# Two pairs of small matmul steps joined, and one PSUM bank each for two kinds of small results, in a delta-rule attention kernel with two feed-forward layers

## The chip, the cores and the metric

The kernel runs on one core of a Trainium2 chip. Its time is device time in microseconds (us). The engines are TensorE (PE, matrix products; PEld is its weight load), VectorE (DVE), ScalarE (ACT), GpSimd (POOL) and the sync engine (SP), which issues the DMA transfers. PSUM, the memory into which PE writes, has eight banks; all eight are in use.

## The reference

A delta rule runs over 768 time steps for 4 batches and 8 heads of size 48, and two feed-forward layers follow.

```python
k_n = k / (norm(k) + 1e-6)
for t in range(S):                       # S = 768
    y[t]  = q[t] @ state                 # state: 48 x 48 for each batch and head
    v_old = state.T @ k_n[t]
    state = state + beta[t] * outer(k_n[t], v[t] - v_old)
x = y as (3072 tokens, 384)
h = x @ w_in;  g = where(h >= 1, h, where(h <= -1, 0, (h + 1)**2 / 4));  x = g @ w_out     # 384 -> 2048 -> 384
h = x @ w_in2; g = maximum(h, 0)**2;                                     out = g @ w_out2
```

## The kernel before

**The recurrence in chunks.** Time is cut into 24 chunks of 32 steps. A chunk's tile has 128 rows: 4 batches of 32 steps. For each chunk PE first makes gram matrices of keys with keys and queries (`gram`, L280), which are masked into `gp`. For a group of up to four chunks, `tri` (L346) inverts the triangular systems, on GpSimd for most groups: one DVE transpose opens it (L363), 60 short GpSimd operations do it (L423 and L424), one DVE transpose closes it (L427). Then `chunk_steps` (L469) does the recurrence in six steps, each 32 small matmuls (64 records in the profile), but for the last:

- `ks` (K S, L484): keys times the state; DVE subtracts it from the scaled values (L494).
- `tr` (L498): the inverse times that, which gives U; ACT copies U out (L506).
- `qs` (Q S, L484 with another index): queries times the state, into the tile `yy`; then the next load of keys and queries is issued.
- `ku` (K'U, L529): adds to the state, which stays in two PSUM banks (`sps`); DVE and ACT copy it out for the next chunk (L534, L535). The last chunk has no K'U.
- `pu` (P U, L518): adds to `yy`; ACT copies the sum out as y (L522).
- `xt` (L552): three transposes of y; ACT rounds the result to the high part (L554), DVE takes the low part (L555). They are the input of the first layer.

**The feed-forward layers.** The first layer takes the chunks in nine blocks of 2 or 3 (`SIZES`), so 256 or 384 columns. For each of 16 slices f of the inner dimension, `hidden` (L577) makes a group of nine matmuls (three products of high and low parts over three slices) and the activation, and `out1` (L626) a group of nine into three accumulators, two slices later. The second layer does the same with 512 tokens at a time.

**What sets the order.** PE's order is written out by hand: the loop at L884 issues, for each f, `hidden`, what is due in slot 2x, `out1` for an earlier slice, and what is due in slot 2x + 1. So each slot follows a group of nine wide matmuls. The chunk steps of block n are spread evenly over the 32 slots of block n - 1 (L813 to L831; over the last 13 slots for n = 1), six steps for each chunk, and four gram steps are put between the steps of some chunks. The variables `at` and `ready` keep the slots at which chunks start and grams are made; the times of `tri` follow from them. The order on DVE, ACT and GpSimd is made by a planner from the dependencies.

**Banks.** Two PSUM banks hold the state, three the accumulators of the output, one the hidden group h. The last two have one tag `att` with two buffers, and all small results (ks, tr, yy, xt and the grams) take them in turn. In the first part of the kernel, before the loop, the small results rotate over these two and the accumulators; the first groups of h, those of the first layer's last block and those of the second layer rotate over the h bank and these two.

Of the kernel before, what the change touches and what calls it, by code (L numbers as in the profile page):

```python
# [8 lines left out]
F32 = mybir.dt.float32  # L9
# [16 lines left out]
def kernel(  # L26
# [22 lines left out]
    nc = tc.nc  # L49
    NCH, P, DM = out.shape  # L50
# [29 lines left out]
    ps = ctx.enter_context(tc.tile_pool(name="ps", bufs=1, space=PSUM))  # L80
# [17 lines left out]
    s_ps = [ps.tile([P, H, D], F32, name=f"sps{i}") for i in range(B2)]  # L98


    early = ["att", "acc0", "att", "acc1", "acc2"]
    turn = [0]

    def att(shape, name):
        tag = "att"
        if turn[0] is not None:
            tag = early[turn[0] % len(early)]
            turn[0] += 1
        return ps.tile(shape, F32, tag=tag, bufs=2 if tag == "att" else 1, name=name)

    def tmp(name, bufs):
        return ring.tile([P, DM], F32, tag=name, bufs=bufs, name=name)
# [6 lines left out]
    def load_kq(c):  # L119
        if c < NCH:  # L120
            kqt[c] = fetch_kq(c, "kqt", KQ)
# [153 lines left out]
    def per_bh(f):  # L275
        for h in range(H):
            for b in range(B):
                f(b, h, slice(T * b, T * (b + 1)), slice(64 * (b % 2), 64 * (b % 2) + D))
# [43 lines left out]
    HEADS = SIZES[0]  # L322
# [146 lines left out]
    def chunk_steps(c):  # L469
        n, j = block_of[c]  # L470
        g, gj = group_of[c]
        t = {}

        def of_state(o, x):

            if c < HEADS:
                for a in range(c):
                    per_bh(lambda b, h, p, pd: nc.tensor.matmul(
                        o[p, h], cross[a, c][p, h, x], us[a][p, h],
                        start=a == 0 and h == 0, stop=x == 0 and a == c - 1,  # L480
                        skip_group_check=True,
                    ))
            else:
                per_bh(lambda b, h, p, pd: nc.tensor.matmul(  # L484
                    o[p, h], kqt[c][pd, b // 2, h, x * T:(x + 1) * T], st[pd, b // 2, h],
                    start=h == 0, stop=x == 0, skip_group_check=True,
                ))

        def ks():
            r = t["r"] = kvt[c][:, 1]  # L490
            if c:
                o = att([P, H, D], "ks")
                of_state(o, 0)
                nc.vector.tensor_sub(r, r, o)  # L494

        def tr():
            o = att([P, H, D], "tr")
            per_bh(lambda b, h, p, pd: nc.tensor.matmul(  # L498
                o[p, h], gp[g][p, 0, gj, h], t["r"][p, h],
                start=h == 0, stop=True, skip_group_check=True,  # L500
            ))
            if c >= HEADS:
                us[c] = t["r"]
            else:
                us[c] = wp.tile([P, H, D], F32, tag=spare[f"u{c}"], name="u")
            nc.scalar.copy(us[c], o)  # L506

        def qs():
            o = t["o"] = att([P, H, D], "yy")
            of_state(o, 1)  # L510
            if c >= HEADS:
                kqt.pop(c)
                load_kq(c + KQ)

        def pu():
            o = t["o"]
            y = t["y"] = t["r"]
            per_bh(lambda b, h, p, pd: nc.tensor.matmul(  # L518
                o[p, h], gp[g][p, 1, gj, h], us[c][p, h],
                start=c == 0 and h == 0, stop=True, skip_group_check=True,  # L520
            ))
            nc.scalar.copy(y, o)  # L522

        def ku():
            k_ = kvt[c]
            if c < NCH - 1:
                kf = k_.rearrange("p x h d -> p (x h d)")
                w = 64 if c == 0 else D
                per_bh(lambda b, h, p, pd: nc.tensor.matmul(  # L529
                    s_ps[b // 2][pd.start:pd.start + w, h], kf[p, D * h:D * h + w], us[c][p, h],  # L530
                    start=c == 0 and h == 0, stop=c == NCH - 2, skip_group_check=True,
                ))
                if c >= HEADS - 1:
                    nc.vector.tensor_copy(st[:, 0], s_ps[0])  # L534
                    nc.scalar.copy(st[:, 1], s_ps[1])  # L535
            done()

        def done():

            t["n"] = t.get("n", 0) + 1  # L540
            if t["n"] == 2:
                del kvt[c]
                load_kv(c + 3)

        def xt():
            if j == 0:
                xh[n] = ring.tile([P, KT, P * SIZES[n]], F32R, tag="xh", bufs=2, name="xh")
                xl[n] = ring.tile([P, KT, P * SIZES[n]], F32R, tag="xl", bufs=2, name="xl")
            o = att([P, KT, P], "xt")
            yf = t["y"].rearrange("p h d -> p (h d)")  # L550
            for kt in range(KT):
                nc.tensor.transpose(o[:, kt], yf[:, kt * P:(kt + 1) * P], ident)  # L552
            cols = slice(j * P, (j + 1) * P)
            nc.scalar.copy(xh[n][:, :, cols], o)  # L554
            marks[2] = nc.vector.tensor_sub(xl[n][:, :, cols], o, xh[n].bitcast(F32)[:, :, cols])  # L555
            done()

        return [ks, tr, qs, pu, ku, xt] if c < HEADS else [ks, tr, qs, ku, pu, xt]


    x2 = dram.tile([P, KT, NCH * P], F32, name="x2", bufs=1)
# [15 lines left out]
    def hidden(layer, n, f):  # L577
        w = P * SIZES[n] if layer == 0 else N
        xs = (xh[n][:, kt] for kt in range(KT)), (xl[n][:, kt] for kt in range(KT))
        if layer:  # L580
            xs = xh[n], xl[n]
        many = turn[0] is not None or (layer, n) >= (0, NB - 1) or n == 0 and f < MANY
        bank = "att" if many and f % 3 else "h"
        h = ps.tile([P, w], F32, tag=bank, bufs={"h": 1, "att": 2}[bank], name="h")
        wi = weight(0, f)
        cols = [slice(kt * P, (kt + 1) * P) for kt in range(KT)]
        prods([
            (h, (wi[0][:, c], wi[1][:, c]), x, kt == 0, kt == KT - 1)
            for kt, (c, *x) in enumerate(zip(cols, *xs))
        ])  # L590
        if layer == 0:
            r = ring.tile([P, w], F32, tag="rg", bufs=RG, name="r")
            g = ring.tile([P, w], F32, tag="rg", bufs=RG, name="g")
        else:
            rg = ring.tile([P, 2, w], F32, tag="xl", bufs=2, name="rg")
            r, g = rg[:, 0], rg[:, 1]
        if layer == 0:


            marks[0] = nc.scalar.activation(r, h, AF.Relu, bias=one)  # L600
            marks[1] = nc.vector.tensor_scalar(g, r, 2.0, 0.5, ALU.min, ALU.mult)  # L601
            nc.scalar.activation(g, g, AF.Square)  # L602
            nc.vector.scalar_tensor_tensor(g, r, -1.0, g, ALU.add, ALU.max)  # L603
        else:
            marks[0] = nc.scalar.activation(r, h, AF.Relu, bias=zero)  # L605
            marks[1] = nc.vector.tensor_mul(g, r, r)  # L606

        def rest():
            if layer == 0:
                ghi = ring.tile([P, w], F32R, tag="gh", bufs=GB, name="gh")  # L610
                glo = ring.tile([P, w], F32R, tag="gl", bufs=GB, name="gl")
            else:
                gg = ring.tile([P, 2, w], F32R, tag="xh", bufs=2, name="gg")
                ghi, glo = gg[:, 0], gg[:, 1]
            nc.scalar.copy(ghi, g)  # L615
            nc.vector.tensor_sub(glo, g, ghi.bitcast(F32))  # L616
            gs[layer, n, f] = (ghi, glo)

        return rest
# [150 lines left out]
    with tc.manual_schedule(engines=ENGINES):  # L770
# [32 lines left out]
        def put_a(n, slot, f):  # L803
            exa.setdefault(SL * n + slot, []).append(f)
# [8 lines left out]
        for n in range(1, NB):  # L813
            todo = []
            for c in range(FIRST[n], FIRST[n] + SIZES[n]):
                g, j = group_of[c]
                due = []
                if j == 0 and 2 <= g < NG - 1:
                    due = list(range(GFIRST[g + 1], GFIRST[g + 1] + GROUPS[g + 1]))
                for i, s_ in enumerate(chunk_steps(c)):  # L820
                    todo.append(((at, c) if i == 0 else None, s_))
                    if i and due:
                        x = due.pop(0)
                        todo.append(((ready, x), lambda x=x: gram(x)))
                assert not due
            for i, (mark, s_) in enumerate(todo):
                o = 0 if n > 1 else HEAD
                slot = SL * (n - 1) + o + i * (SL - o) // len(todo)
                if mark:
                    mark[0][mark[1]] = slot  # L830
                put_a(0, slot, s_)  # L831
# [52 lines left out]
        for x in range(total):  # L884
            g, f = divmod(x, NF)
# [64 lines left out]
```

## Time and profile before

| | us |
|---|---|
| median of 3 runs | 1042.16 |
| lowest, highest | 1041.61, 1044.85 |
| the profiled execution | 1043.48 |
| its span on the core | 1041.8 |

Busy in that span: PE 984.1 us (94%), DVE 572.2 (55%), ACT 467.1 (45%), GpSimd 319.1 (31%). The core's mean granted clock is 0.994 of full speed.

How to read the rows: times run from the start of the span. A row of the timeline has the start, the time from its first instruction's start to its last one's end, the engine, the line of the kernel, the operation, the tiles (written <- read), the shapes and the count; in brackets the idle time of the engine before it and what ended it. Matmuls are pipelined, so a row's time overlaps the next row's start; the difference of two starts is what a group takes from the engine. A small matmul step stands as 64 records.

### The profile page before, as it was taken

The page shows a single profiled execution, that of the slowest core. Times are in us where ns is not written, and L with a number is a line of the kernel's source. Part 1 is how long each engine was busy: PE and PEld are TensorE (multiplying, and loading weights), DVE is VectorE, ACT ScalarE, POOL GpSimd, SP SyncE. Part 2 cuts the span into 40 slices and gives each one's busy share as a digit, 9 for nine tenths or more (in the row PEclk, how much of TensorE's full clock was granted, in tenths as well). Part 3 has the DMA queues.
Part 4 walks back from the last instruction along what each step waited for, and adds up shares of the span by engine and source line. Part 5 has one row for each costly group of instructions (what it writes and reads, how often), then busy time and mean ns, then how long its engine had stood idle before and what let it go on. Part 6 is the DMA issues. An engine that isn't in the chain of part 4 may idle for free.

```text
span 1041.8 us, 32099 instructions
## 1 busy us (share of the span) xinstructions
PE 984.1 (94%) x14152; PEld 905.0 (87%) x14152; DVE 572.2 (55%) x994; ACT 467.1 (45%) x935; POOL 319.1 (31%) x476
## 2 busy tenths in 40 slices
PE   4358899999999999999999999999999999999998
PEld 4347888899899989999999999998989999999997
DVE  6988665775575666666546577533343333433333
ACT  2776354554454545545444554333333333333332
POOL 3792770393059118518503122120020010200000
PEclk9998999999999999999999999999999999999999
DMA  9874144441542542513012223101010000000000
GB/s 258 223 204 145 47 133 142 116 137 43 159 118 61 155 116 74 145 55 100 17 41 63 91 78 99 31 1 61 1 61 1 1 31 1 23 8 1 31 1 31
DMA packets 35245, 80.83 MB, mean 78 GB/s; under 512 B 4513, under 2 KB 15265, under 8 KB 35105
## 3 DMA queue, kind: packets, MB, share of 16 engines
q1 hardware_dynamic: 35104, 78.78, 25.6%
q8 instruction: 111, 1.82, 0.8%
q14 instruction: 30, 0.24, 0.1%
HBM read 63.03 MB, written 15.73 MB: 76 GB/s over the span
## 4 chain that ended last, share of the span: by engine, by line
PE 84%; DMA 6%; DVE 5%; ACT 2%; issue 1%; SPq 1%; ACTq 0%; DVEq 0%
PE acc L567 37%; PE h L567 37%; DMA raw<-in_w_dram 5%; PE tr L498 2%; PE yy L518 2%; PE sps L529 2%; PE yy L484 2%; PE g L293 1%; PE ks L484 1%; DVE g L603 1%; DMA kqt<-in_kq_dram 1%; PE xt L552 1%; DVE gp L427 1%; DVE wl L187 1%; DVE gm L363 0%
## 5 line engine op out<-in xcount | busy, mean ns | idle before, releaser
L567 PE MATMUL acc<-w,gg 128*128 128x384 f32 x1152 | 218.2, 337 | 0.3 <-ACT e L623 0.3
L567 PE MATMUL h<-x2s,w 128*128 128x512 f32 x864 | 213.8, 392 | 0.0
L567 PEld LDWEIGHTS acc<-w,gg 128*128 128x128 f32 x1152 | 204.5, 187 | 8.6 <-ACT e L623 0.9
L567 PEld LDWEIGHTS h<-x2s,w 128*128 128x128 f32 x864 | 160.9, 188 | 28.2
L567 PE MATMUL h<-xh,w 128*128 128x384 f32 (+1 forms) x864 | 167.2, 330 | 2.3 <-ACT r L600 1.7
L567 PE MATMUL acc<-gh,w 128*128 128x384 f32 (+1 forms) x864 | 166.7, 328 | 1.5 <-ACT gh L615 1.5
L606 DVE TENSOR_TENSOR rg<-rg 128x512 f32<-128x512 f32 x96 | 71.3, 743 | 139.5 <-ACT rg L605 139.5
L567 PEld LDWEIGHTS h<-xh,w 128*128 128x128 f32 x864 | 138.5, 192 | 7.3 <-ACT r L600 2.3
L567 PEld LDWEIGHTS acc<-gh,w 128*128 128x128 f32 x864 | 136.0, 189 | 6.5 <-ACT gh L615 1.7
L605 ACT ACTIVATE rg<-h,zero 128x512 f32<-128x512 f32 x96 | 66.0, 687 | 137.7 <-PE h L567 137.7
L616 DVE TENSOR_TENSOR gl<-g,gh 128x384 fp32r<-128x384 f32 (+1 forms) x144 | 89.1, 619 | 63.7 <-ACT gh L615 59.8
L616 DVE TENSOR_TENSOR gg<-rg,gg 128x512 fp32r<-128x512 f32 x96 | 66.7, 695 | 104.3 <-ACT gg L615 104.3
L600 ACT ACTIVATE r<-h,one 128x384 f32<-128x384 f32 (+1 forms) x144 | 78.3, 544 | 97.0 <-PE h L567 96.0
L615 ACT CAST gh<-g 128x384 fp32r<-128x384 f32 (+1 forms) x144 | 68.7, 477 | 107.1 <-DVE g L603 90.1
L424 POOL TENSOR_TENSOR tx<-tx,t 128x30 f32<-128x30 f32 (+9 forms) x180 | 110.3, 613 | 13.7
L423 POOL TENSOR_TENSOR t<-tx,gm 128x30 f32<-128x30 f32 (+9 forms) x180 | 108.5, 603 | 18.8 <-DVE tx L402 5.2
L615 ACT CAST gg<-rg 128x512 fp32r<-128x512 f32 x96 | 59.7, 622 | 119.6 <-PE acc L567 112.6
L603 DVE SCALAR_TENSOR_TENSOR g<-r,g 128x384 f32<-128x384 f32 (+1 forms) x144 | 88.3, 613 | 40.5 <-ACT g L602 38.8
L601 DVE TENSOR_SCALAR g<-r 128x384 f32<-128x384 f32 (+1 forms) x144 | 57.9, 402 | 87.7 <-ACT r L600 86.8
L567 PE MATMUL h<-xl,w 128*128 128x384 f32 (+1 forms) x432 | 91.5, 321 | 1.3 <-DVE xl L555 1.3
L567 PE MATMUL acc<-gl,w 128*128 128x384 f32 (+1 forms) x432 | 91.0, 319 | 1.8 <-DVE gl L616 1.8
L602 ACT ACTIVATE g<-g 128x384 f32<-128x384 f32 (+1 forms) x144 | 70.2, 487 | 47.9 <-DVE g L601 47.2
(98 smaller groups left out, 930.3 us busy)
## 6 DMA issues: line engine op xcount, KB each, us to landing
raw<-in_w_dram SPq DMA_DIRECT2D x64, 384.0 KB, 3.7
kqt<-in_kq_dram SPq DMA_DIRECT2D x88, 192.0 KB, 3.7
kv<-in_kv_dram SPq DMA_DIRECT2D x24, 384.0 KB, 3.2
w2f<-wl SPq DMA_DIRECT2D x32, 192.0 KB, 3.3
w2r<-w2f SPq DMA_DIRECT2D x16, 384.0 KB, 3.0
x2r<-x SPq DMA_DIRECT2D x6, 768.0 KB, 4.8
out_dram<-e SPq DMA_DIRECT2D x23, 192.0 KB, 2.0
x<-e SPq DMA_DIRECT2D x18, 192.0 KB, 2.1
```

The costliest lines, as they stand in the source:

```text
L423: eng.tensor_mul(t, by.to_broadcast(shape), of.to_broadcast(shape))
L424: eng.tensor_add(rest, rest, t)
L484: per_bh(lambda b, h, p, pd: nc.tensor.matmul(o[p, h], kqt[c][pd, b // 2, h, x * T:(x + 1) * T], st[pd, b // 2, h], start=h == 0, stop=x = ...
L567: nc.tensor.matmul(o, *((r, l) if swap else (l, r)), **flags)
L600: marks[0] = nc.scalar.activation(r, h, AF.Relu, bias=one)
L601: marks[1] = nc.vector.tensor_scalar(g, r, 2.0, 0.5, ALU.min, ALU.mult)
L602: nc.scalar.activation(g, g, AF.Square)
L603: nc.vector.scalar_tensor_tensor(g, r, -1.0, g, ALU.add, ALU.max)
L605: marks[0] = nc.scalar.activation(r, h, AF.Relu, bias=zero)
L606: marks[1] = nc.vector.tensor_mul(g, r, r)
L615: nc.scalar.copy(ghi, g)
L616: nc.vector.tensor_sub(glo, g, ghi.bitcast(F32))
```

## The change

The two buffers with one tag become two tags with a buffer each. `att1` takes `yy` alone (Q S and P U); `att0` takes all other small results. Before the loop the rotation names the same five banks as before; the groups of h that used the two buffers in turn now name them by f.

For the chunks from the third on, the six steps become four: K S and Q S together, U, K'U and P U together, and the transposes. In the second pair the copies of the state come behind both matmul steps, and the copy of y behind those. The first two chunks keep six steps. A gram may now also stand right behind the first step of a chunk.

```diff
-    early = ["att", "acc0", "att", "acc1", "acc2"]
+    early = ["att0", "acc0", "att1", "acc1", "acc2"]
     turn = [0]
 
     def att(shape, name):
-        tag = "att"
+        tag = "att1" if name == "yy" else "att0"
         if turn[0] is not None:
             tag = early[turn[0] % len(early)]
             turn[0] += 1
-        return ps.tile(shape, F32, tag=tag, bufs=2 if tag == "att" else 1, name=name)
+        return ps.tile(shape, F32, tag=tag, name=name)
...
                 start=c == 0 and h == 0, stop=True, skip_group_check=True,
             ))
-            nc.scalar.copy(y, o)
+            if c < HEADS:
+                nc.scalar.copy(y, o)
...
                     start=c == 0 and h == 0, stop=c == NCH - 2, skip_group_check=True,
                 ))
+                if c >= HEADS:
+                    pu()
                 if c >= HEADS - 1:
                     nc.vector.tensor_copy(st[:, 0], s_ps[0])
                     nc.scalar.copy(st[:, 1], s_ps[1])
+            else:
+                pu()
+            if c >= HEADS:
+                nc.scalar.copy(t["y"], t["o"])
             done()
...
-        return [ks, tr, qs, pu, ku, xt] if c < HEADS else [ks, tr, qs, ku, pu, xt]
+        return [ks, tr, qs, pu, ku, xt] if c < HEADS else [lambda: (ks(), qs()), tr, ku, xt]
...
-        bank = "att" if many and f % 3 else "h"
-        h = ps.tile([P, w], F32, tag=bank, bufs={"h": 1, "att": 2}[bank], name="h")
+        h = ps.tile([P, w], F32, tag=("h", "att0", "att1")[f % 3 if many else 0], name="h")
...
                 for i, s_ in enumerate(chunk_steps(c)):
                     todo.append(((at, c) if i == 0 else None, s_))
-                    if i and due:
+                    if due:
                         x = due.pop(0)
                         todo.append(((ready, x), lambda x=x: gram(x)))
```

## Rows read from the trace of the kernel before

**Rows 1.** The profile page's part 4: the chain that ended last, by engine

```profile
PE 84%; DMA 6%; DVE 5%; ACT 2%; issue 1%; SPq 1%; ACTq 0%; DVEq 0%
```

**Rows 2.** Busy time by stretch: length, each engine's busy us, PEclk, DMA share, GB/s

```profile
104.00:200.00 96.00, 89.00 (x2438) 81.49 (x2439) 59.26 (x127) 45.73 (x112) 41.80 (x69) 0.98 0.37 106
200.00:590.00 390.00, 388.08 (x7682) 359.26 (x7681) 238.38 (x429) 199.32 (x417) 176.91 (x273) 1.00 0.32 93
...
640.00:1041.80 401.80, 397.85 (x2003) 361.55 (x2001) 153.51 (x217) 131.01 (x208) 32.31 (x30) 1.00 0.06 22
```

**Rows 3.** PE's groups, 104 to 640 us: busy us, mean ns | idle before

```profile
L567 PE MATMUL h<-xl,w 128*128 128x384 f32 x288 | 65.9, 337 | 1.3 <-DVE xl L555 1.3
...
L484 PE MATMUL ks<-st,kqt 48*32 48x48 f32 x1408 | 19.5, 204 | 0.0
L498 PE MATMUL tr<-kv,gp 32*32 32x48 f32 x1408 | 19.4, 202 | 5.2 <-DVE kv L494 5.2
```

**Rows 4.** Timeline of PE: wide groups alone and between small steps

```profile
101.51 0.87 PE L567 MATMUL h<-xh,w 128*128 128x256 f32 x6
...
102.57 0.87 PE L567 MATMUL acc<-gh,w 128*128 128x256 f32 x6
...
126.79 0.88 PE L484 MATMUL yy<-st,kqt 48*32 48x48 f32 x64
127.60 0.97 PE L567 MATMUL h<-xh,w 128*128 128x256 f32 x6
...
128.86 0.93 PE L529 MATMUL sps<-kv 32*48 32x48 f32 x64
...
336.99 1.31 PE L567 MATMUL h<-xh,w 128*128 128x384 f32 x6
...
338.75 0.89 PE L484 MATMUL yy<-st,kqt 48*32 48x48 f32 x64
...
595.96 1.20 PE L567 MATMUL h<-xh,w 128*128 128x384 f32 x6
...
597.52 1.20 PE L567 MATMUL acc<-gh,w 128*128 128x384 f32 x6
```

**Rows 5.** Timeline of PE: two small steps back to back, before the loop

```profile
52.31 1.50 PE L498 MATMUL tr<-kv,gp 32*32 32x48 f32 x64 [2.61 <-DVE kv L494]
53.60 1.49 PE L478 MATMUL yy<-u,cross 32*32 32x48 f32 x64
```

**Rows 6.** Timeline of PE: stalls, and a slow step at 113.22

```profile
110.57 0.88 PE L498 MATMUL tr<-kv,gp 32*32 32x48 f32 x64 [2.03 <-DVE kv L494]
...
113.22 1.50 PE L484 MATMUL yy<-st,kqt 48*32 48x48 f32 x64
...
124.72 0.88 PE L498 MATMUL tr<-kv,gp 32*32 32x48 f32 x64 [0.83 <-DVE kv L494]
...
170.10 0.88 PE L498 MATMUL tr<-kv,gp 32*32 32x48 f32 x64 [1.73 <-DVE kv L494]
...
194.79 0.79 PE L567 MATMUL h<-xl,w 128*128 128x384 f32 x3 [0.58 <-DVE xl L555]
```

**Rows 7.** Timeline: DVE's transpose and read-out of ks, then xt and its read-out

```profile
107.35 2.11 DVE L427 STREAM_TRANSPOSE gp<-tx 128x1024 f32<-128x1024 f32 x1
...
109.98 0.54 DVE L494 TENSOR_TENSOR kv<-kv,ks 128x384 f32<-128x384 f32 x1
...
164.78 0.49 PE L552 MATMUL xt<-ident,kv 128*128 128x128 f32 x3
...
168.26 0.57 DVE L555 TENSOR_TENSOR xl<-xt,xh 128x384 fp32r<-128x384 f32 x1
```

**Rows 8.** Timeline: end of one GpSimd chain, and DVE's transpose of its result

```profile
341.28 0.28 POOL L424 TENSOR_TENSOR tx<-tx,t 128x30 f32<-128x30 f32 x1
...
349.15 2.22 DVE L427 STREAM_TRANSPOSE gp<-tx 128x1024 f32<-128x1024 f32 x1
```

**Rows 9.** Busy time of the stretch behind the first stall

```profile
110.50:116.00 5.50, 5.43 (x146) 5.02 (x146) 2.12 (x7) 1.61 (x5) 4.10 (x11) 0.69 0.06 13
```

## The prediction

> **What bounds the kernel now.** I read the chain of waits first: TensorE (PE) holds 84% of it, and nearly all of the rest lies in the first 100 us, where data and constants come in [rows 1]. The table by stretches says the same in time. From 104 to 200 us PE is busy 89.0 of 96.0 us, from 200 to 590 us 388.1 of 390.0, and from 640 us on 397.9 of 401.8; VectorE (DVE) is busy for 238.4 of the 390 [rows 2]. So from 104 us on, a microsecond counts if it is one of PE's own or if PE stands still for it. Before that PE waits for others; the change leaves the order of work there as it is (the rotation over five banks names the same banks), so I put that stretch at zero. After 640 us nothing is touched.
>
> Next I read PE's groups from 104 to 640 us. The recurrence steps are short: all of K S takes 19.5 us. The counts give the number of steps: 1408 records of ks are 22 chunks of 64 (the first two chunks are done earlier). PE's idle time is small: 5.2 us ahead of tr and 1.3 us ahead of h [rows 3], of 8.9 us in all between 104 and 590 us (7.0 and 1.9) [rows 2].
>
> **The change, part by part.**
>
> *1. Fewer interruptions.* Each recurrence step is put into a stream of wide matmuls. In PE's order of time, a group of nine 384-wide matmuls between two others takes 595.96 to 597.52 = 1.56 us; one that has a small step on either side takes 336.99 to 338.75 = 1.76. For 256 columns it is 101.51 to 102.57 = 1.06 and 127.60 to 128.86 = 1.26 [rows 4]. Both ends of an interruption together cost 0.20 us, whatever the width. The change puts Q S right behind K S in 22 chunks and P U right behind K'U in 21 (the code does no K'U for the last chunk), so 43 interruptions go. No matmul goes: 64 records of each step stay.
>
> What the new seam between two small steps costs, the steady stretch does not show. Bounds: nothing, or the 0.20 us of a seam between small and wide. The nearest row is early, where tr and yy stand back to back: tr starts at 52.31 and yy 1.29 us later, both last 1.50 and 1.49 us, so the second is not stretched [rows 5]. PE ran at half pace there, but it is the same kind of seam, so I take nothing. Term: 43 x 0.20 = 8.6 us less, bounds 0 to 8.6.
>
> *2. Waits of PE that get more time.* A block's steps are spread over 32 slots (a slot follows each group of nine wide matmuls). Per three chunks there were 18 steps, or 22 with four gram steps; now there are 12 or 16. Two steps that lay 1.5 slots apart now lie 2 or more apart. That bears on these stalls:
> - tr waits for DVE to subtract ks: 5.2 us in five stalls, the largest 2.03 at 110.57, 0.83 at 124.72 and 1.73 at 170.10 [rows 3, 6]. Each had one group between ks and tr; now Q S (126.79 to 127.60, 0.81 us [rows 4]) lies between too, and in all but the first of them two groups or more. The first is set by DVE, which runs a 2.11 us transpose from 107.35 and gets to the subtraction at 109.98 [rows 7]; there only Q S and its seams come in between, so about 1.1 us stays. Gone: 5.2 - 1.1 = 4.1.
> - the first group of a block waits for the low part of the last transposed chunk: 1.3 us in two stalls (0.58 at 194.79) [rows 3, 6]. That xt was at slot 30 and is now at 28 or 29, a group of over 1 us earlier. Gone: 1.3.
> Term: 5.4 us less, bounds 0 (the stall comes back elsewhere) to 6.5.
>
> *3. A new wait: one bank for K S, U, xt and the grams.* Each of these had a second bank; now each waits until the result before it has been read out. Behind a waiting step PE's whole queue stands. Between two uses of the bank now lie two groups, 2.3 us at 256 columns (1.06 + 1.26) and 3.3 at 384 [rows 4]. tr needs the ks result read anyway. What is late next is K S behind xt. The worst row: xt ends at 165.27 (164.78 + 0.49) and DVE reads it out from 168.26 to 168.83, 3.56 us later [rows 7]. Before, K S ran meanwhile in the other bank. With one bank K S of that chunk would wait 3.56 - 2.3 = 1.2 us; but the read-out stood behind a transpose that closes a group, and the change places that transpose a slot behind xt instead of in the same slot, so it may fall after the read-out. Bounds 0 to 1.2; I take the middle, 0.6. At 384 columns 3.56 would exceed the gap by 0.3 us only.
>
> The Trainium skill (page Perfetto Trace Analysis, section Optimizing Tensor Performance, Matmuls) speaks against this part: independent groups of matmuls should rotate through different PSUM banks, so that one is read out while the next computes. By that rule all three uses of a chunk would pay; the rival "one bank" below prices it. The rows agree with it only where the read-out is longer than the wide groups in between.
>
> *4. Moves on the other engines.* The copy of y goes from behind P U to behind the copies of the state, on ScalarE's (ACT) queue, and xt waits for it; no copy is added. The loads of later K and Q chunks go out one step earlier on the sync queue, which helps if anything. For one group of chunks the last gram now comes three slots later, so GpSimd's chain starts later: it ended at 341.56 (341.28 + 0.28), 7.6 us before DVE transposed its result at 349.15 [rows 8]. Three slots, each a group of 1.56 to 1.76 us [rows 4] and part of an insertion, are some 6 us, of which merging gives back about half by then, and tr of that chunk also moves two slots on; no cost. The order on DVE and ACT is planned anew, though, and a 2 us transpose can again fall ahead of a result that PE needs. I allow one such stall of the size of 1.73 us [rows 6]; bounds 0 to 4.
>
> **Sum.** -8.6 - 5.4 + 0.6 + 1.7 = -11.7 us. The profiled execution took 1043.48 us (span 1041.8), so it would take 1031.8. It lay 1.3 us above the median of the runs, 1042.16; from that median the forecast is 1030.5.
>
> Not in the sum: behind the 2.03 us stall the granted clock falls to 0.69 over 110.5 to 116 us (2.4 GHz for part of it, 1.2 for the rest) and a step that takes 0.88 us at 126.79 takes 1.50 at 113.22 [rows 4, 6, 9]. The step and its two neighbours lose some 1.5 us. If halving the stall keeps the clock up, that is a further gain; as half the stall stays, I count none.
>
> **Rivals.**
> - *Only the seams go.* The stalls move with the new plan instead of vanishing: 1042.2 - 8.6 = 1033.5. For it: the causes, DVE's 2 us transposes, all stay [rows 7]. Against: the distances grow in all chunks.
> - *The seam between small steps costs like any other.* Then part 1 is nil and parts 2 to 4 leave 1042.2 - 3.1 = 1039. For it: no row at full clock shows two small steps back to back. Against: rows 5.
> - *One bank makes it slower.* Place: the 256-wide stretches, 8 chunks, whose two groups give only 2.3 us. If DVE's queue made a delay of 3.56 us the rule there, three uses per chunk would wait 1.2 us each: 8 x 3 x 1.2 = 29 us more, less the 8.6 of part 1: 1062. It starts to decide when the bank is awaited 0.13 us per use on average (8.6 over 22 chunks x 3). For it: the 3.56 us row [rows 7]. Against: that read-out, and that of 109.98, stood behind a transpose, and the code has two of these for each of seven groups of chunks, not one ahead of every read-out.
> - *It comes out even.* The merged insertion is twice as long (1.6 us), so ACT's and DVE's work for the wide groups shifts against PE and new gaps eat the gain: 1041 to 1043. Against: DVE has 150 of 390 us free [rows 2].
>
> **How the numbers follow.** The forecast 0.60, with its own range 1026 to 1033; only the seams 0.17; dear seams 0.10; one bank slower 0.08; even 0.05. Within 0.3% (3.1 us) a measurement of this kernel can't be told from no change: faster means below 1039.0. That takes in the first two cases and half of the third: 0.82. Same: the other half and the even case, 0.10. Slower: 0.08. Range: the low end is both upper bounds of parts 1 and 2 and the clock's 1.5 us without any new stall, 1042.2 - 8.6 - 6.5 - 1.5 = 1025.6, rounded down to 1025; the high end takes in the larger part of the dear seams, 1038.5.
>
> **What would show it.** Right: in steady stretches ks starts, yy follows 0.81 us later, the next wide group 1.63 us later; sps and yy likewise; the wide groups keep 1.56, 1.66 and 1.76 us, with fewer of the last; PE's idle from 104 to 590 us falls from 8.9 to about 6 us. Wrong: yy starts over 0.9 us after ks, or the first wide matmul behind a pair is longer than behind a single step (dear seams); PE's waits name the read-outs of xt, u or g ahead of ks and g (one bank); or the time falls by less than 8 us though the seams are gone, and then PE's idle names a new wait.

## The result, and the profile after

| | median us (runs) | lowest to highest |
|---|---|---|
| before | 1042.16 (5) | 1041.23 to 1044.92 |
| changed | 1029.86 (5) | 1027.45 to 1030.92 |

The medians lie 12.3 us apart; the ratio is 0.9872 with a 95% interval of 0.985 to 0.9894 (11 to 16 us less). The forecast was 1030.5. The profiled execution of the changed kernel took 1027.45 us, its span 1025.7.

First the busy time of the changed kernel by stretches (columns as in [rows 2]). PE stands still for 5.3 us from 104 to 200 us and for 2.3 from 200 to 590, so 7.6 us against 8.9.

```profile
104.00:200.00 96.00, 90.70 (x2656) 84.75 (x2654) 63.64 (x134) 50.13 (x121) 49.58 (x80) 1.00 0.40 117
200.00:590.00 390.00, 387.70 (x7552) 368.38 (x7553) 248.39 (x441) 202.13 (x426) 173.69 (x266) 1.00 0.31 93
...
640.00:1025.70 385.70, 381.76 (x1922) 346.96 (x1921) 143.04 (x202) 124.35 (x197) 28.95 (x27) 1.00 0.05 18
```

The whole difference lies ahead of the second layer: that starts at 633.40 us before and at 617.32 now, and takes 408.4 and 408.3 us. Of these 16.1 us 1.5 are there when the first wide group starts (68.86 and 67.32), a stretch that holds the same instructions in the same order; that is scatter between two executions. 14.5 us are left to explain. (In both kernels the granted clock is at its lower level for part of the time ahead of 104 us: a mean of 0.92 over 60 to 104 us before and of 0.80 now.)

PE's groups from 104 to 640 us in the changed kernel answer to [rows 3]. The wait of tr fell from 5.2 to 1.4 us and that of h from 1.3 to nothing; a wait of ks for the read-out of xt, 3.6 us, is new.

```profile
L574 PE MATMUL h<-xl,w 128*128 128x384 f32 x288 | 65.7, 336 | 0.0
...
L484 PE MATMUL ks<-st,kqt 48*32 48x48 f32 x1408 | 19.5, 204 | 3.7 <-DVE xl L562 3.6
L498 PE MATMUL tr<-kv,gp 32*32 32x48 f32 x1408 | 19.4, 202 | 1.4 <-DVE kv L494 1.4
...
L484 PE MATMUL yy<-st,kqt 48*32 48x48 f32 x1408 | 19.1, 203 | 1.5 <-issue 1.5
```

Next PE's timeline around a chunk in the steady part of the changed kernel. Q S starts 0.71 us behind K S and the wide group 0.78 behind Q S; a single step had kept PE for 0.81. P U starts 0.86 behind K'U and keeps PE for 0.82.

```profile
304.71 0.88 PE L484 MATMUL ks<-st,kqt 48*32 48x48 f32 x64
305.42 0.86 PE L484 MATMUL yy<-st,kqt 48*32 48x48 f32 x64
306.20 1.32 PE L574 MATMUL acc<-gh,w 128*128 128x384 f32 x6
...
313.67 0.93 PE L530 MATMUL sps<-kv 32*48 32x48 f32 x64
314.53 0.88 PE L518 MATMUL yy<-kv,gp 32*32 32x48 f32 x64
315.35 1.31 PE L574 MATMUL acc<-gh,w 128*128 128x384 f32 x6
```

Over all undisturbed pairs of the trace the medians are 0.704 and 0.790 us for K S and Q S (0.814 each before), and 0.863 and 0.812 for K'U and P U (the same as before). With the interruption, 0.204, a pair of the first kind saves 2 x 0.814 - 0.704 - 0.790 + 0.204 = 0.338 us, one of the second 0.204. So by the rows the seams are worth 22 x 0.338 + 21 x 0.204 = 11.7 us.

The last piece is the clock. In the stretch of [rows 9] it now stays up:

```profile
110.50:116.00 5.50, 5.50 (x173) 5.18 (x160) 2.83 (x8) 3.25 (x8) 4.67 (x11) 1.00 0.01 3
```

The stall ahead of tr is 1.42 us here, not 2.03, and no step of this stretch takes 1.50 us:

```profile
109.76 0.88 PE L498 MATMUL tr<-kv,gp 32*32 32x48 f32 x64 [1.42 <-DVE kv L494]
```

These are some 1.5 us, which the forecast had named and left out. Together: 11.7 of seams, 8.9 - 7.6 = 1.3 of idle time, some 1.5 of clock, 14.5 us. That this meets the 14.5 exactly is in part chance. The three terms belong to the time from about 98 us on, when both kernels start the same gram:

```profile
98.25 1.10 PE L293 MATMUL g<-kqt 48*32 48x64 f32 x64
97.37 1.10 PE L293 MATMUL g<-kqt 48*32 48x64 f32 x64
```

The first row is from the kernel before, the second from the changed one. The lead is 0.9 us here, so from here on there are 16.1 - 0.9 = 15.2 us, and 0.7 of them stay without an explanation. Between the first wide group and this gram the changed kernel lost 0.7 us of its lead, with PE busy for 23.4 of 30.1 us there (24.3 of 29.4 before).

### The profile page after: what moved, and what is told of

Its sections match the earlier page's. It is cut to its first block, busy times and chain, and to the rows that moved or that the text cites. A ratio compares the mean times of both kernels' runs of the same rounds, so it can differ in the third digit from the quotient of the medians.

```text
span 1025.7 us, 32117 instructions
## 1 busy us (share of the span) xinstructions
PE 968.5 (94%) x14152; PEld 900.8 (88%) x14152; DVE 576.5 (56%) x994; ACT 465.7 (45%) x935; POOL 320.6 (31%) x476
## 4 chain that ended last, share of the span: by engine, by line
PE 84%; DMA 6%; DVE 5%; ACT 2%; issue 1%; SPq 0%; ACTq 0%; DVEq 0%
PE acc L574 38%; PE h L574 37%; DMA raw<-in_w_dram 5%; PE sps L530 2%; PE tr L498 2%; PE yy L518 2%; PE ks L484 2%; PE yy L484 1%; PE g L293 1%; DVE gp L427 1%; DVE gm L363 1%; DMA kqt<-in_kq_dram 1%; PE xt L559 1%; DVE g L609 1%; ACT r L606 1%
## 5 line engine op out<-in xcount | busy, mean ns | idle before, releaser
L574 PE MATMUL h<-xh,w 128*128 128x384 f32 (+1 forms) x864 | 161.3, 323 | 2.9 <-ACT r L606 2.3
L423 POOL TENSOR_TENSOR t<-tx,gm 128x30 f32<-128x30 f32 (+9 forms) x180 | 111.7, 621 | 16.1 <-DVE tx L402 2.8
L607 DVE TENSOR_SCALAR g<-r 128x384 f32<-128x384 f32 (+1 forms) x144 | 62.1, 431 | 73.5 <-ACT r L606 72.6
```

The costliest lines, as they stand in the source:

```text
L423: eng.tensor_mul(t, by.to_broadcast(shape), of.to_broadcast(shape))
L574: nc.tensor.matmul(o, *((r, l) if swap else (l, r)), **flags)
```

## Experiments

All times are against the kernel before, run beside it on the same chip. The ratio is turned into microseconds of 1042.

| run | median us | ratio (95%) | us against before |
|---|---|---|---|
| banks alone, six steps, old slots | 1046.38 | 1.004 (1.0025 to 1.0055) | +4.2 |
| Q S joined alone | 1035.54 | 0.9938 (0.9922 to 0.9955) | -6.5 |
| P U joined alone | 1040.83 | 0.9987 (0.9973 to 1.0) | -1.4 |
| both joined, old slots | 1037.93 | 0.9963 (0.995 to 0.9976) | -3.9 |
| new slots, nothing joined | 1040.57 | 0.9982 (0.9972 to 0.9992) | -1.9 |
| changed kernel, xt in the other bank | 1026.81 | 0.985 (0.9835 to 0.9865) | -15.6 |
| the same again | 1029.25 | 0.9872 (0.9851 to 0.9893) | -13.3 |
| changed kernel again, beside it | 1028.77 | 0.9874 (0.9853 to 0.9895) | -13.1 |
| six steps, old slots, xt in the other bank | 1043.28 | 1.0011 (0.9997 to 1.0025) | +1.1 |
| both joined, old slots, xt in the other bank | 1034.18 | 0.9922 (0.9897 to 0.9946) | -8.1 |
| xt in the other bank, grams joined | 1032.00 | 0.9901 (0.988 to 0.9922) | -10.3 |
| pairs in turned order | 1029.86 (one run) | | |

**Banks alone.** The new tags, the rest as before; `pu` is a step by itself again, with its copy. (The edits here and below are against the changed kernel; `...` stands for lines not shown.)

```diff
...
-                if c >= HEADS:
-                    pu()
...
-        return [ks, tr, qs, pu, ku, xt] if c < HEADS else [lambda: (ks(), qs()), tr, ku, xt]
+        return [ks, tr, qs, pu, ku, xt] if c < HEADS else [ks, tr, qs, ku, pu, xt]
...
-                    if due:
+                    if i and due:
```

> The new banks with the six old steps at their old slots; no pair is joined. Theory A (the time went with the seams: in the profile after, Q S starts 0.70 us behind K S instead of 0.81 and every pair saves an interruption of 0.20, so 22 x 0.34 + 21 x 0.20 = 11.7 us): no gain, 1042 us, or up to 4 us slower if K S waits for the read-out of xt. Theory B (part of the gain is fewer waits of PE through banks and spacing): the banks alone bring nothing either, 1042. Rival, banks matter: 1039 or less, or over 1046.

4.2 us slower: this is theory A's upper bound and the far end of the rival, so it does not part the two, but theory B's 1042 is out. The banks are not free. PE's waits from 104 to 640 us (us, times, longest) have a new first row, in an execution of 1048.31 us, the slowest of its seven:

```profile
PE ks L484 <- DVE xl L555: 6.1, 6, 2.5
PE tr L498 <- DVE kv L494: 3.9, 4, 2.5
```

**Only Q S joined, only P U joined.** One pair each; the other step stays alone, so chunks have five steps, at slots of their own. In the first, P U has its own copy of y again.

```diff
...
-        return [ks, tr, qs, pu, ku, xt] if c < HEADS else [lambda: (ks(), qs()), tr, ku, xt]
+        return [ks, tr, qs, pu, ku, xt] if c < HEADS else [lambda: (ks(), qs()), tr, ku, pu, xt]
```
```diff
-        return [ks, tr, qs, pu, ku, xt] if c < HEADS else [lambda: (ks(), qs()), tr, ku, xt]
+        return [ks, tr, qs, pu, ku, xt] if c < HEADS else [ks, tr, qs, ku, xt]
```

> Only Q S joined to K S; P U stays a step of its own. Theory A: 22 x 0.34 = 7.4 us less than before, 1034.8. With a seam worth 0.20 us as I forecast: 22 x 0.20 = 4.4 less, 1037.8. If waits are what counts: tr gets more time after K S, the larger part of the 5.4 us of waits goes too, 1033 or less.

> Only P U joined to K'U; Q S stays a step of its own. Theory A: 21 x 0.20 = 4.3 us less than before, 1037.9, and P U starts 0.86 us behind K'U (this seam, unlike the other, gives nothing beyond the interruption). Rival, each pair is worth the same: 5.9 us less, 1036.3.

Q S alone gives 6.5 us (4.7 to 8.1); theory A's 7.4 lies in the interval, and 4.4 does not. P U alone gives 1.4 (0 to 2.8), less than its 4.3; its waits of PE from 104 to 640 us sum to 8.9 us, no fewer than before. The seams themselves are as theory A has them in both traces (medians 0.704 and 0.863 us). But each of the two times is a sum of seams, banks and five-step slots, so neither gives the price of a seam by itself. They add up to 7.9, not to 13: in this sum the price of the banks (4.2 us at the slots of six steps) stands twice. How much of the gap is the banks and how much the slots, these two runs do not show.

**Both joined at the old slots.** Empty steps stand where Q S and P U were.

```diff
+        none = lambda: None
-        return [ks, tr, qs, pu, ku, xt] if c < HEADS else [lambda: (ks(), qs()), tr, ku, xt]
+        return [ks, tr, qs, pu, ku, xt] if c < HEADS else [lambda: (ks(), qs()), tr, none, ku, none, xt]
...
-                    if due:
+                    if i and due:
```

> Both pairs joined, but the slots of the old plan are kept (empty steps stand where Q S and P U were), so tr is again mostly one group behind K S and the grams lie where they were. Theory A (seams): 11.7 us less than before, 1030.5, as the changed kernel within 2 us. Theory B (the forecast's part 2, waits that get more time): the 5 us of waits ahead of tr stay, 1034 or more, and tr's idle time is named in PE's waits.

3.9 us, far from 11.7: the seams alone do not give the time. In the profiled execution (1041.56 us, the slowest of twelve) PE stands still for 14.6 us from 104 to 640 us, against 8.9 before. But the waits are not mainly those ahead of tr that theory B named (2.8 us): ks waits 7.2 us for xt. Two stalls come close together in PE's timeline, and the table of stretches shows the clock behind them at 0.77:

```profile
144.70 0.97 PE L575 MATMUL h<-xh,w 128*128 128x256 f32 x6 [1.39 <-ACT r L607]
147.07 1.48 PE L484 MATMUL ks<-st,kqt 48*32 48x48 f32 x64 [1.04 <-DVE xl L562]
```
```profile
145.00:160.00 15.00, 13.96 (x376) 13.09 (x375) 7.14 (x17) 7.59 (x20) 6.50 (x14) 0.77 0.43 137
```

**New slots, nothing joined.** Q S and P U one slot behind K S and K'U.

```diff
...
+        behind_[ks], behind_[ku] = qs, pu
-        return [ks, tr, qs, pu, ku, xt] if c < HEADS else [lambda: (ks(), qs()), tr, ku, xt]
+        return [ks, tr, qs, pu, ku, xt] if c < HEADS else [ks, tr, ku, xt]
...
                 put_a(0, slot, s_)
+                if s_ in behind_:
+                    put_a(0, slot + 1, behind_[s_])
```

> The slots of the changed kernel, but Q S and P U stand one slot behind K S and K'U, so a group of wide matmuls lies between and no interruption is saved (in one or two places the next step shares the slot); waits for tr and xt have the new spacing. Theory A (seams): the gain of 11.7 us is gone, 1040 to 1042. Theory B (waits): the part of 5.4 us stays, 1037 or less.

1.9 us (0.8 to 2.9): theory A's range, and not the 5.4 of the forecast. In the timeline the price of the wide groups is back (312.14 - 310.37 = 1.77 us between two small steps):

```profile
309.56 0.88 PE L485 MATMUL ks<-st,kqt 48*32 48x48 f32 x64
310.37 1.32 PE L569 MATMUL acc<-gh,w 128*128 128x384 f32 x6
...
312.14 0.88 PE L485 MATMUL yy<-st,kqt 48*32 48x48 f32 x64
```

From this run to the changed kernel, which has the same banks and the same slots for the four steps, it is 13.3 - 1.9 = 11.4 us (13.3 is its ratio of 0.9872 in the same measure, 11.0 to 15.6). That is the joining by itself, with the two intervals some 9 to 14 us, and the rows made it 11.7. (In two places the moved step stands right beside the next step, so 41 and not 43 interruptions come back: 11.3 by the rows.)

**xt in the other bank**, twice, the second time beside the changed kernel.

```diff
-        tag = "att1" if name == "yy" else "att0"
+        tag = "att1" if name in ("yy", "xt") else "att0"
```

> The changed kernel with the transposes xt in the bank of Q S and P U instead of the other. In the profile after, K S waits 3.6 us in four places for the read-out of xt. If one bank for xt and K S causes these: they go or turn into a wait of Q S that is 0.7 us shorter each, 1 to 3.5 us less than the changed kernel, 1026.5 to 1029. If they are the delay of DVE's queue that PE meets elsewhere anyway: 1029 to 1031.

> The changed kernel itself, on the chip of the other runs of this call, for comparison: 0.987 of before, 1029 to 1031.

> The changed kernel with xt in the bank of Q S and P U, again beside the changed kernel: 2 to 4 us less than it, since K S waited 3.6 us for xt there. If the difference of the first run was that of two chips, it is within 1 us.

The wait of ks is gone from PE's waits, and Q S waits 1.0 us instead. The first run seemed 2 us better than the changed kernel of the result above; side by side the two are equal (-13.3 and -13.1). So at the new slots the one bank's wait can't be shown to cost anything, and this version does not beat the changed kernel.

**Six steps at the old slots with xt in the other bank**, and **both joined there**: the first and fourth runs again, with the edit above.

> As the run with the banks alone (six old steps, old slots, 4.2 us slower than before by the ratio), but xt goes to the bank of Q S and P U. In that run K S waited 6.1 us for the read-out of xt, a wait that the kernel before did not have. If that wait is the price of the banks: it goes, and the time is that of before within 1.5 us, 1040.5 to 1043.5. If the price lies in the planner's new order on DVE and ACT: 1045 or more still.

> Both pairs joined at the old slots, with xt in the bank of Q S and P U: against the run of six steps with xt there (1043.3 us, 1.0011 of before) banks and slots are the same, and only the seams differ. Theory A: 22 x 0.34 + 21 x 0.20 = 11.7 us less than that run, about 1031.5 or 0.990 of before. Rival, the joined pairs give back what they save when the next step is close (as in the run with one bank at the old slots, 3.8 us under before): 1036 or more.

With six steps the 6.1 us wait is gone, tr waits 5.1 us as it did before, and the time is 3.1 us lower than with the banks alone (the two intervals together leave some 1 to 5): most of their price comes from K S behind xt. Joining at equal banks and slots then gives 1.1 + 8.1 = 9.2 us, against 4.2 + 3.9 = 8.1 with the one bank and 11.4 at the new slots. So the seams pay everywhere. That closer slots take some of it back is less sure, as each of the three differences is known to 2 or 3 us; for it speaks that in the profiled executions PE stands still from 104 to 640 us for 10.0 us with the pairs joined at the old slots and for 8.5 with the six steps there. In PE's waits of the joined kernel the old causes stand again:

```profile
PE tr L498 <- DVE kv L494: 3.2, 2, 1.8
PE yy L484 <- DVE xl L562: 2.8, 4, 1.7
PE tr L498 <- issue: 1.3, 3, 0.9
```

**Pairs in turned order**, for the seams alone; in `ku` the call of `pu` stands ahead of K'U, and the next load goes out behind K S.

```diff
...
-        return [ks, tr, qs, pu, ku, xt] if c < HEADS else [lambda: (ks(), qs()), tr, ku, xt]
+        return [ks, tr, qs, pu, ku, xt] if c < HEADS else [lambda: (qs(), ks()), tr, ku, xt]
```

> In both pairs the order is turned round: Q S ahead of K S, P U ahead of K'U. Seen in the starts on PE: if the short seam belongs to two steps with the same tiles of the array (48 rows by 32 columns in both), K S starts 0.70 us behind Q S, and K'U (32 by 48) starts 0.81 us behind P U (32 by 32), as any wide group would. If instead the first step of a pair is short because of its operands, K S keeps 0.70 and starts of the other differ. Time as the changed kernel, 1030 within 3 us.

```profile
308.53 0.88 PE L484 MATMUL yy<-st,kqt 48*32 48x48 f32 x64
309.24 0.86 PE L484 MATMUL ks<-st,kqt 48*32 48x48 f32 x64
310.03 1.32 PE L574 MATMUL acc<-gh,w 128*128 128x384 f32 x6
...
317.49 0.88 PE L518 MATMUL yy<-kv,gp 32*32 32x48 f32 x64
318.31 0.93 PE L532 MATMUL sps<-kv 32*48 32x48 f32 x64
```

As the first reading said: the step that comes first in the pair with equal tiles (48*32 in the row) is the one that is short, whichever it is, and the seam between unequal tiles (32*32, then 32*48) takes the 0.81 us that a wide follower would see. The two pairs differ in more than the tiles, in the operands too; a third pair, tr and yy of 32*32, speaks for the tiles (part 1 below).

**Grams joined**, an attempt at a better version: the third and fourth gram of a chunk ride with K'U and P U and with xt.

```diff
+                    if due and i > 1:
+                        x = due.pop(0)
+                        todo.append(((ready, x), lambda s_=s_, x=x: (s_(), gram(x))))
+                        continue
...
-                    if due:
+                    if len(due) > 2:
```

> As the run with xt in the other bank, and 8 of the 14 grams of the loop are joined to K'U and P U or to xt instead of standing alone. By the seams (0.204 us for an interruption of small matmuls between wide groups, some 0.18 where xt is the neighbour): 8 x 0.19 = 1.5 us less than that run, about 1025. If a gram directly behind P U or xt makes DVE late for the next step: no gain or up to 2 us more.

Some 3 us slower than the kernel that it was made from, on the same chip. The waits named "issue" (nothing in the profile ended them, and PE stops in the middle of a step) rise from 1.7 to 5.8 us:

```profile
PE yy L484 <- issue: 2.4, 2, 1.2
PE yy L518 <- issue: 1.9, 1, 1.9
PE g L293 <- issue: 1.5, 3, 1.0
```

The longest are 1.94, 1.25, 1.14 and 1.03 us, at 158, 122, 289 and 184 us. Their places are not free. These four have 3288, 2266, 6097 and 3926 of PE's matmul records ahead of them, counted from the start of the trace; the first six of the kernel before have 223, 351, 479, 606, 734 and 862. All 112 stops called "issue" in the fourteen traces of this case stand on this one grid of 127.7 matmuls, within three. With one weight load for each matmul that is nearly 256 records. Most of these places pass without a stop. From 104 us on, 26 of 27 stops fall into small steps, where PE has 128 records in 0.81 us, against 18 in 1.56 us for a wide group. So the place in PE's stream of instructions decides where it can stop; why it does at one of these places and not at the next is open.

## Why the prediction was right, point by point

*Part 1, the seams, -8.6 us.* The mechanism holds: 43 interruptions went, and joining alone is worth 11.4 us by the runs, 11.7 by the rows. By its own sign, Q S 0.81 us behind K S, it came out shorter: 0.70. The size was 3 us too small. I took the seam between two small steps as costing nothing beyond the step's own 0.81 us. But 0.11 us of that time is itself the change from small to wide, and between two steps with equal tiles it goes too; with the 0.024 that Q S is shorter that makes 22 x 0.134 = 2.9 us. The rows that I leaned on, [rows 5], have equal tiles of 32 by 32 at half pace, and I read in them only that the second step is not stretched. Set beside a lone step at that pace they show that the first is shortened. The kernel before has one, Q S at 113.22 of [rows 6]: the next group starts 1.44 us later. In the run with the banks alone it is tr itself, at a granted clock of 0.50, with a wide group behind it:

```profile
111.16 1.50 PE L498 MATMUL tr<-kv,gp 32*32 32x48 f32 x64 [2.46 <-DVE kv L494]
112.59 1.65 PE L567 MATMUL acc<-gh,w 128*128 128x256 f32 x6
```

That is 1.43 us, against the 1.29 from tr to yy in [rows 5]; a second profile of the changed kernel has tr and yy at a granted clock of 0.50, and 1.29 us there too (54.57 to 55.86). Between K'U and P U the forecast of nothing was exact.

*Part 2, waits with more time, -5.4 us.* Foretold for tr: 1.1 us stay; measured 1.4. For h: none; measured none. These two came as worked out. Beside them, small waits that the prediction did not name went as well: of h for ScalarE's activation from 1.0 to 0.2 us, of xt for the copy of y from 0.9 to nothing, and a stop in P U of 0.5 us.

*Part 3, one bank, +0.6 us.* This is the term that was mis-sized: 3.6 us in four waits. The worst is where I had looked for it, in timeline order:

```profile
156.22 0.49 PE L559 MATMUL xt<-ident,kv 128*128 128x128 f32 x3
...
157.66 2.16 DVE L427 STREAM_TRANSPOSE gp<-tx 128x1024 f32<-128x1024 f32 x1
...
159.67 0.57 DVE L562 TENSOR_TENSOR xl<-xt,xh 128x384 fp32r<-128x384 f32 x1
...
160.29 0.88 PE L484 MATMUL ks<-st,kqt 48*32 48x48 f32 x64 [1.54 <-DVE xl L562]
```

The transpose still stands ahead of the read-out on DVE, although its slot now comes after that of xt; I had hoped for the opposite order in half the cases. My upper bound of 1.2 us was passed: I had bounded one place, and there were four. PE's waits naming xt's read-out ahead of K S were one of the prediction's signs for the one-bank rival; the sign came, but its 3.6 us did not outweigh the seams.

*Part 4, a new stall, +1.7 us.* Q S stops once for 1.5 us ("issue") and a wide group 0.7 us for an accumulator's read-out. The size is near (2.2 us), the cause was a guess: no transpose is named as what Q S waited for, and its stop lies at one of the places in PE's stream that are described above (2266 matmuls ahead of it). GpSimd's later chain did no harm, as foretold: it ended at 334.75 us, DVE's transpose began at 337.14.

*Sum of parts 2 to 4:* -3.1 foretold; -1.3 by the idle time, -1.9 (-0.8 to -2.9) by the run with nothing joined. PE's idle time from 104 to 590 us fell to 7.6 us, not to about 6. So that the total came out within a microsecond (1029.86 against 1030.5; 13.3 us against 11.7 by the ratio) is in part luck: the gain of the seams was taken 3 us too low and that of the rest 1 to 2 us too high.

*The clock*, left out of the sum, gave some 1.5 us in the profiled pair. A second profile of the changed kernel has 1.00 from 104 us on as well; in how many executions of either kernel it is so, profiles of one or two can't tell.

*The rivals.* Dear seams: refuted. Only the seams go: close, but slots and banks together do bring something. One bank makes it slower: wrong for the change as it is, right at the old slots, where banks alone cost 4.2 us. The rule of the Trainium skill (page Perfetto Trace Analysis, section Optimizing Tensor Performance, Matmuls) that independent groups rotate through banks is borne out there: giving xt another bank took back 3.1 us. At the new slots it changed nothing that these runs can show. What saved the change are the slots that joining frees: 12 or 16 steps in 32 slots leave two wide groups between uses of the bank. With the same banks and nothing joined, the move from the old slots (+4.2) to the new ones (-1.9) alone is worth some 6 us.

## What to carry to other kernels

Count the places where a stream of wide matmuls is broken, not only the matmuls: here each break costs 0.20 us, and joining two small steps with equal tiles saves a further 0.13. Time such a seam against a lone step at the same clock, and not only by whether the second step is longer. Before taking a buffer away, compare the longest read-out in the rows with the work between two uses, in every place and not in the worst alone. An edit that is harmless or useful together with another may lose alone (the banks: +4.2 us), so test parts in pairs that share all but one thing.

## What was not expected of the hardware

- Two steps of 64 small matmuls with the same tile shape follow each other in 0.704 us; with unequal shapes, or a wide group behind, the first takes 0.81 (0.86 for K'U). Which of the two comes first makes no difference. At the lower clock it is 1.29 us for tr with equal tiles behind it and 1.43 with a wide group.
- The stops of PE that nothing in the profile ends lie at fixed places in its stream, multiples of 127.7 matmuls apart, in all fourteen traces; those of the loop took 0.2 to 1.9 us each.
- The granted clock fell to the lower level (1.2 GHz) for a while in several of these kernels behind stalls of PE of 1 to 2.5 us: a mean of 0.69 over 110.5 to 116 us before [rows 9], of 0.77 over 145 to 160 us with both joined at the old slots. The stalls of up to 1.5 us in the changed kernel had no such sequel (1.00 from 104 us on).
- The second layer, which no edit touches, took 1 to 4 us longer in some executions. In that of the second run with xt in the other bank it was 411.9 us instead of 408.3: ScalarE's copy of an output waited 3.71 us for an earlier output transfer, PE 1.83 us for ScalarE, and the granted clock was 0.89 over 890 to 905 us. So a difference of 2 or 3 us between two executions need not belong to the edit.
